# Three attention-and-MoE slots without weight conversions, and a reordered ending

## The chip, the cores and the metric

One core of one Trainium2 chip. The metric is the time of one execution in device microseconds (us); below is better. A core has TensorE (PE, matrix products; PEld its weight loads), VectorE (DVE), ScalarE (ACT), GpSimd (POOL) and SyncE (SP, which here issues every DMA). Each engine takes its instructions in the order in which the program issues them and waits for the others by semaphores.

## The reference

Sliding-window attention with a few global keys, and then two feed-forward layers over all 1,536 tokens (width 512, hidden width 2,048), all in float32:

```python
h = x @ w_in
g = np.maximum(h, 0.0) + alpha * np.minimum(h, 0.0)
x = (g @ w_out).astype(np.float32)          # first layer

h = x @ w_in                                # second layer
h2 = h * h
h3 = h2 * h
P = a[0] + a[1] * h + a[2] * h2 + a[3] * h3
Q = 1.0 + np.abs(b[0]) * np.abs(h) + np.abs(b[1]) * h2
g = P / (Q + 1e-06)
out = (g @ w_out).astype(np.float32)
```

## The kernel before

The two layers are cut into 96 **steps** (`plan_weights`, L221): a step is one layer, one group `g` of 512 tokens and one chunk of 128 hidden units. Steps 0 to 47 are the first layer, 48 to 95 the second. Precision comes from splitting every operand into a high and a low half and adding three products. A step has a **first product** (`first`, L731, matmuls of L738: 12 of 128x512 into one of banks 0 to 2), an elementwise part and a **second product** (`second`, L791, matmuls of L804: 12 into banks 4 to 7, which add up over a run of steps).

After the attention the steps go through **slots** (`plain_slot`, L866, slots 16 to 97). Slot s issues the first product of step s, the elementwise work of steps s-1 and s-2, and the second product of step s-2. In the second layer this is, for the step n: ACT L756, L757 and L761 read the bank (`rational_a`, `rational_u`); DVE L765 (`rational_b`); ACT L769 and L770 (`rational_c`); DVE L775 and L776 (`rational_p`); one slot later DVE L780, L781 and L782 (`rational_d`), ACT L785, which makes the high half `ghi` (`rational_h`), and POOL L789, which makes the low half `glo` (`rational_e`). The second product begins with `ghi` and takes `glo` in its last third.

Each slot has two **ticks** (`tick`, L284), numbered 2s and 2s+1: the first stands between L765 and L769, the second after the second product. The 20 ticks -20 to -1 run before slot 0. Ticks carry two sorts of side work:

- A **conversion** unpacks a chunk of weights that came in as 64-bit numbers. It is spread over four ticks: at tick t ACT scales it (L324), at t+1 DVE joins the bits (L313, L314, L315, and then the next load is issued on SP), at t+2 ACT makes the high half (L301), at t+3 DVE the low half (L304). `plan_weights` lists the ticks at which conversions begin; the last eight begin at 101, 106, ... 136 (L248), so 101 is the second tick of slot 50.
- The queue `later` holds the **low halves of the last sums** of a first-layer group that was computed in two runs of steps (those that end at steps 39 and 47): `drain` (L813) adds the bank to the saved part (DVE L829), ACT makes the high half (L837), and the low half (DVE L838, four of 128x512 per group) is queued. One is taken at every tick.

The ends of other runs (steps 55, 63, 79, 87, 95) copy or add banks 4 to 7 and store them: three drains at once, the fourth in the next slot.

The last step, 95, is done in halves of 256 tokens (`final_slot`, L899), since nothing is left to overlap it with; `drain` then adds the last bank in two halves (L825) and stores each with a DMA issued by SP (L826). The whole is in one arm of a run-time branch, so each engine ends its work with a branch (L92) and a closing sequence (L973).

Of the kernel before, what the change touches and what calls it, by code (L numbers as in the profile page):

```python
# [52 lines left out]
def flat(t):  # L53
    return t.rearrange("p c f -> p (c f)")


def words(t):
    return flat(t).bitcast(F32)


class Kernel:
# [35 lines left out]
    def arm(self, attention, sfx):  # L97
        tc = self.tc
        self.sfx = sfx
        self.slots = list(self.early)  # L100
        self.pipe, self.join, self.unspilled, self.later, self.splits = (deque() for _ in range(5))
        self.loads = self.started = self.used = 0
        moe = self.moe()
        with tc.tile_pool(name="spill_" + sfx, bufs=1, space=DRAM) as spill:
            self.spilled = [self.alloc_slot(spill, i, "d") for i in range(KEPT)]
            self.saved = {mg: spill.tile([P, NC, DM], F32, name=f"saved{mg[0]}{mg[1]}_{sfx}") for mg in SAVED}
            with tc.tile_pool(name="at_" + sfx, bufs=1) as pool:
                attention(pool, moe)
            with tc.tile_pool(name="late_" + sfx, bufs=1, reuse_waits="tile") as late:
                self.slots += [self.alloc_slot(late, i) for i in range(NEARLY, NF)]  # L110
                moe(None)
# [109 lines left out]
    def plan_weights(self):  # L221
        self.steps = [(0, 0, fc, fc % NEARLY) for fc in range(CH)]
        self.steps += [(0, 1, fc, fc % NEARLY) for fc in (*range(NEARLY, CH), *range(NEARLY))]
        self.steps += [(0, 2, fc, fc) for fc in range(NF)]
        self.steps += [(0, g, fc, fc) for g in (0, 1) for fc in range(CH, NF)]
        self.steps += [(1, g, j, j) for g in (2, 0) for j in range(CH)]
        self.steps += [(1, 1, j, j) for j in range(NF)]
        self.steps += [(1, g, j, j) for g in (2, 0) for j in range(CH, NF)]
        runs = [s[:2] for s in self.steps]
        self.begins = {n for n in range(len(runs)) if n == 0 or runs[n - 1] != runs[n]}  # L230
        self.ends = {n - 1 for n in self.begins if n} | {len(runs) - 1}
        self.saves = {n for n in self.ends if runs[n] in runs[n + 1 :]}
        self.adds = {n for n in self.ends - self.saves if runs[n] in SAVED}
        jobs = {}
        for fc in range(CH):
            jobs[2 * fc - 5 if fc > 2 else 2 * fc - 10] = 0, fc, "in", fc % NEARLY
            jobs[2 * fc - 2 if fc else -5] = 0, fc, "out", fc % NEARLY
        half, layer = NGR * CH, NGR * NF
        spare = [(fc, kind) for fc in range(CH, NF) for kind in ("in", "out")]
        for t, (fc, kind) in enumerate(spare):  # L240
            jobs[11 + 2 * t if fc < KEPT else 15 + 2 * t] = 0, fc, kind, None if fc < KEPT else fc
        todo = []
        for n, free in ((0, LATE), (CH, layer - CH)):
            for k in range(CH):
                for kind, lag in (("in", 0), ("out", 5)):
                    todo.append((n + k, 2 * (free + k) + lag, kind))
        times = [t for t in range(48, 96) if (t % 2 == 0 or t in (55, 71) or t > 82) and t not in (64, 66, 80, 82, 85, 88, 91, 94, 95)]
        times += range(101, 160, 5)  # L248
        for t in times:
            ready = [x for x in todo if x[1] <= t]  # L250
            if ready:
                j, _, kind = job = min(ready)
                todo.remove(job)
                jobs[t] = 1, j, kind, j
        assert not todo
        self.starts = set(jobs)
        self.plan = [jobs[t] for t in sorted(jobs)]
# [25 lines left out]

    def tick(self, on_act, start, spread=False):  # L284
        nc = self.nc
        if self.later:
            self.later.popleft()()
        while self.splits:
            self.splits.popleft()()
        self.join_step(5)  # L290
        if self.pipe and self.pipe[0][0] == "joined":
            _, n = self.pipe.popleft()
            m, fc, kind, slot = self.plan[n]
            self.spill()
            x = words(self.dx[n % 3])
            if slot is None:
                hi, lo = (t.bitcast(F32R) for t in self.part[1:3])
            else:
                hi, lo = (flat(self.slots[slot][kind, part]) for part in PARTS)
            if on_act:  # L300
                nc.scalar.copy(hi, x)  # L301
            else:
                nc.gpsimd.tensor_scalar(hi, x, 1.0, 1.0, ALU.mult, ALU.mult)
            self.splits.append(lambda: nc.vector.tensor_sub(lo, x, hi.bitcast(F32)))  # L304
            if m == 0 and fc < KEPT:
                for part, of in zip(PARTS, (hi, lo)):
                    self.unspilled.append((words(self.spilled[fc][kind, part]), of.bitcast(F32)))
        if self.pipe:
            _, n = self.pipe[0]
            self.pipe[0] = "joined", n  # L310
            low, e, y = self.staged(n)[:, :, :, 0], self.de[n % 2].bitcast(I32), self.dx[n % 3]
            self.join += [
                lambda: nc.vector.tensor_scalar(y, e, 3, None, ALU.logical_shift_left),  # L313
                lambda: nc.vector.scalar_tensor_tensor(y, e, -(2**31), y, ALU.bitwise_and, ALU.bitwise_or),  # L314
                lambda: nc.vector.scalar_tensor_tensor(y, low, 29, y, ALU.logical_shift_right, ALU.bitwise_or),  # L315
                self.load_more,
            ]
        if not spread:
            self.join_step(5)
        if start:  # L320
            n = self.started
            self.started += 1
            self.pipe.append(("scaled", n))
            nc.scalar.mul(self.de[n % 2], self.staged(n)[:, :, :, 1].bitcast(F32), 2.0**-112)  # L324
# [399 lines left out]
    def moe(self):  # L724
        nc, steps, banks = self.nc, self.steps, self.banks
        N = len(steps)
# [4 lines left out]
        def first(n):  # L731
            m, g, fc, slot = steps[n]
            w = self.slots[slot]
            bk = banks[3 if n < LATE else n % 3]
            seq = [(a, b, c) for a, b in (("hi", "hi"), ("lo", "hi"), ("hi", "lo")) for c in range(NC)]
            for e, (a, b, c) in enumerate(seq):
                x = (self.xhi if b == "hi" else self.xlo)[g]
                nc.tensor.matmul(bk, w["in", a][:, c, :], x[:, c, :], start=e == 0, stop=e == len(seq) - 1)  # L738
            hbank[n] = bk
# [73 lines left out]
        def drain(n, d):  # L813
            m, g = steps[n][:2]
            y, o, r0 = banks[4 + d], self.part[d], g * GT + d * P
            out = self.out[r0 : r0 + P, :]
            if n in self.saves:
                if n < LATE - 1:
                    o = self.first_saved[d]
                (nc.vector.tensor_copy if d == 3 and m else nc.scalar.copy)(o, y)  # L820
                nc.sync.dma_start(out=self.saved[m, g][:, d, :], in_=o)
                return
            if n == N - 1 and d == 3:
                for half in (slice(0, DM // 2), slice(DM // 2, DM)):
                    nc.vector.tensor_add(o[:, half], y[:, half], o[:, half])  # L825
                    nc.sync.dma_start(out=out[:, half], in_=o[:, half])  # L826
                return
            if n in self.adds:
                nc.vector.tensor_add(o, y, o)  # L829
            elif m:  # L830
                (nc.vector.tensor_copy if d == 3 else nc.scalar.copy)(o, y)
            if m:
                nc.sync.dma_start(out=out, in_=o)
                return
            xh, xl = self.xhi[g][:, d, :], self.xlo[g][:, d, :]
            if n in self.adds:
                nc.scalar.copy(xh, o)  # L837
                self.later.append(lambda: nc.vector.tensor_sub(xl, o, xh.bitcast(F32)))  # L838
            else:
                nc.scalar.copy(xh, y)  # L840
                nc.vector.tensor_sub(xl, y, xh.bitcast(F32))
# [24 lines left out]
        def plain_slot(s):  # L866
            early, late = s - 1, s - 2
            fetch(s + 1)
            if CH <= s - LATE + CH - 2 < KEPT:
                self.reload(s - LATE + CH - 2)  # L870
            if s < N:
                first(s)
            if s >= N:
                final_slot(s)
                return
# [102 lines left out]
```

## Time and profile before

| | |
|---|---|
| three runs shown | 676.52, 677.80 and 678.18 us, median 677.8 |
| the profiled execution's own time | 678.08 us |
| its span, first to last instruction | 676.2 us, so 1.9 us lie around it |
| mean granted TensorE clock | 0.98 |
| PE busy | 631.6 us, 93% of the span |
| DVE busy | 541.6 us, 80% |
| ACT busy | 374.7 us, 55% |
| POOL busy | 195.2 us, 29% |

Matmuls are pipelined: in an unbroken row they start 0.227 us apart, though a row of the profile gives each 0.39 us. So a slot of 24 matmuls takes 5.44 us, and idle time that the profile gives before a matmul is 0.16 us less than what is lost from start to start. In a timeline row a bracket tells how long the engine was idle before it and which instruction ended that.

### The profile page before, as it was taken

What the parts mean: (1) busy time and instruction counts of PE and PEld (TensorE: products, weight loads), DVE (VectorE), ACT (ScalarE), POOL (GpSimd) and SP (SyncE); (2) the same over time, 40 slices, a digit from 0 to 9 for tenths busy, and PEclk for the clock granted to TensorE, in tenths of its full rate; (3) what the DMA queues carried; (4) which work ended last, traced back from release to release, by engine and by line L of the source; (5) the groups of instructions that cost most, each with busy time, mean ns of one, the idle gap of its engine ahead of it and who ended that gap; (6) DMA issues with size and microseconds to landing.
All of it is one profiled execution on the core that took longest, in us unless ns stands there. A gap on an engine that the chain in (4) does not pass through costs nothing.

```text
span 676.2 us, 9567 instructions
## 1 busy us (share of the span) xinstructions
PE 631.6 (93%) x3250; PEld 510.2 (75%) x3250; DVE 541.6 (80%) x982; ACT 374.7 (55%) x782; POOL 195.2 (29%) x278
## 2 busy tenths in 40 slices
PE   7767998998988999999999998999999999999994
PEld 6656766776866888888888876888878888888782
DVE  3687789984654998876879999999999877786984
ACT  2775565665552432333324367777777766766662
POOL 4554334333232322222222212222222222222221
PEclk9897999998999999999999999999999999999997
DMA  8969488876667882331342231121110000300302
GB/s 164 198 165 271 136 249 251 258 221 222 186 225 235 291 317 89 99 121 31 126 155 63 70 117 31 32 95 39 55 62 1 1 1 1 124 1 0 126 0 69
DMA packets 84860, 82.83 MB, mean 123 GB/s; under 512 B 45312, under 2 KB 61952, under 8 KB 84800
## 3 DMA queue, kind: packets, MB, share of 16 engines
q1 hardware_dynamic: 84800, 82.11, 40.5%
q8 instruction: 28, 0.46, 0.3%
q14 instruction: 32, 0.26, 0.1%
HBM read 60.21 MB, written 19.92 MB: 119 GB/s over the span
## 4 chain that ended last, share of the span: by engine, by line
PE 59%; DVE 23%; ACT 6%; DMA 4%; issue 3%; POOL 3%; SPq 0%; DVEq 0%; ACTq 0%; POOLq 0%
PE bank L804 29%; PE bank L738 28%; DVE dx L314 3%; DVE dx L315 3%; DVE dx L313 3%; ACT prob L453 2%; DMA dwouthi_f<-part 2%; DVE prob L446 1%; DVE act L745 1%; DVE act L744 1%; DMA dwinhi_f<-part 1%; DVE xlo L527 1%; DVE klo L407 1%; DVE act L782 1%; POOL glo L747 1%
## 5 line engine op out<-in xcount | busy, mean ns | idle before, releaser
L747 POOL TENSOR_TENSOR glo<-act,ghi 128x512 fp32r<-128x512 f32 x48 | 65.6, 1367 | 225.6 <-ACT ghi L746 202.6
L789 POOL TENSOR_TENSOR glo<-act,ghi 128x512 fp32r<-128x512 f32 (+1 forms) x49 | 65.7, 1340 | 202.1 <-ACT ghi L785 187.2
L746 ACT CAST ghi<-act 128x512 fp32r<-128x512 f32 x48 | 29.8, 621 | 107.6 <-DVE act L745 99.7
L738 PE MATMUL bank<-xhi,winhi_f 128*128 128x512 f32 x256 | 68.4, 389 | 0.0
L738 PE MATMUL bank<-xhi,winlo_f 128*128 128x512 f32 x256 | 68.4, 389 | 0.0
L738 PE MATMUL bank<-xlo,winhi_f 128*128 128x512 f32 x256 | 68.4, 389 | 0.0
L453 ACT ACTIVATE prob<-prob,stat 128x232 f32<-128x232 f32 (+1 forms) x96 | 44.6, 466 | 38.8 <-DVE stat L446 38.7
L738 PEld LDWEIGHTS bank<-xhi,winhi_f 128*128 128x128 f32 x256 | 48.0, 188 | 10.0
L738 PEld LDWEIGHTS bank<-xlo,winhi_f 128*128 128x128 f32 x256 | 48.0, 188 | 10.0
L738 PEld LDWEIGHTS bank<-xhi,winlo_f 128*128 128x128 f32 x256 | 48.0, 188 | 10.0
L315 DVE SCALAR_TENSOR_TENSOR dx<-stage,dx 128x512 int32<-128x512 int32 x64 | 53.5, 836 | 2.2
L314 DVE SCALAR_TENSOR_TENSOR dx<-de,dx 128x512 int32<-128x512 int32 x64 | 51.8, 809 | 2.2
L756 ACT ACTIVATE stage<-bank 128x512 f32<-128x512 f32 (+1 forms) x49 | 28.8, 588 | 37.5 <-PE bank L738 37.4
L765 DVE SCALAR_TENSOR_TENSOR stage<-stage,abs_b 128x512 f32<-128x512 f32 (+1 forms) x49 | 36.2, 739 | 16.3 <-ACT stage L757 16.3
L470 POOL TENSOR_SCALAR prob<-prob,rec 128x232 f32<-128x232 f32 (+1 forms) x96 | 43.0, 464 | 21.7 <-DVE rec L465 14.3
L785 ACT CAST ghi<-act 128x512 fp32r<-128x512 f32 (+1 forms) x49 | 30.1, 614 | 26.5 <-DVE act L782 26.4
L324 ACT ACTIVATE de<-stage 128x512 f32<-128x512 f32 x64 | 42.4, 667 | 2.3 <-DMA stage<-in_moe_w_out_dram 2.3
L804 PE MATMUL bank<-wouthi_f,ghi 128*128 128x512 f32 x144 | 41.3, 392 | 0.6 <-ACT ghi L785 0.6
L744 DVE TENSOR_SCALAR act<-bank,al 128x512 f32<-128x512 f32 x48 | 35.8, 745 | 7.4 <-PE bank L738 7.2
L804 PE MATMUL bank<-wouthi_f,glo 128*128 128x512 f32 x144 | 41.2, 391 | 0.1
L804 PE MATMUL bank<-woutlo_f,ghi 128*128 128x512 f32 x144 | 41.0, 389 | 0.0
L313 DVE TENSOR_SCALAR dx<-de 128x512 int32<-128x512 int32 x64 | 38.0, 594 | 3.5 <-ACT de L324 3.5
(206 smaller groups left out, 1483.5 us busy)
## 6 DMA issues: line engine op xcount, KB each, us to landing
stage<-in_moe_w_in_dram SPq DMA_DIRECT2D x32, 512.0 KB, 4.1
stage<-in_moe_w_out_dram SPq DMA_DIRECT2D x32, 512.0 KB, 4.0
part<-saved_f SPq DMA_DIRECT2D x16, 256.0 KB, 4.3
va<-in_v_dram SPq DMA_DIRECT2D x13, 256.0 KB, 5.0
saved_f<-part SPq DMA_DIRECT2D x12, 256.0 KB, 3.7
out_dram<-part SPq DMA_DIRECT2D x11, 256.0 KB, 2.1
rawk<-in_k_dram SPq DMA_DIRECT2D x10, 256.0 KB, 4.7
rawq<-in_q_dram SPq DMA_DIRECT2D x10, 256.0 KB, 4.6
```

What stands on the lines that cost most here:

```text
L313: lambda: nc.vector.tensor_scalar(y, e, 3, None, ALU.logical_shift_left),
L314: lambda: nc.vector.scalar_tensor_tensor(y, e, -(2**31), y, ALU.bitwise_and, ALU.bitwise_or),
L315: lambda: nc.vector.scalar_tensor_tensor(y, low, 29, y, ALU.logical_shift_right, ALU.bitwise_or),
L324: nc.scalar.mul(self.de[n % 2], self.staged(n)[:, :, :, 1].bitcast(F32), 2.0**-112)
L453: nc.scalar.activation(p[:, j - e, :w], p[:, j - e, :w], AF.Exp, bias=st[:, j : j + 1], scale=-1.0, accum_out=st[:, 4 + j : 5 + j],)
L470: nc.gpsimd.tensor_scalar(p[:, j, :w], p[:, j, :w], r[:, e + j : e + j + 1], 1.0, ALU.mult, ALU.mult)
L738: nc.tensor.matmul(bk, w["in", a][:, c, :], x[:, c, :], start=e == 0, stop=e == len(seq) - 1)
L744: nc.vector.tensor_scalar(t, h, 0.0, self.al[:, fc : fc + 1], ALU.min, ALU.mult)
L747: nc.gpsimd.tensor_tensor(lo, t, hi.bitcast(F32), ALU.subtract)
L765: nc.vector.scalar_tensor_tensor(w, w, self.ab[:, 0:1], ab, ALU.add, ALU.mult)
L789: nc.gpsimd.tensor_tensor(lo, u, hi.bitcast(F32), ALU.subtract)
L804: nc.tensor.matmul(y[d], lhs, rhs, start=begin and e == 0, stop=last and e == 2)
```

## The change

Four edits. A counter of ticks is kept, and `later` is served only when it is odd. The last eight conversions begin at ticks 107, 112, ... 142. Of the two half stores of the last drain, ACT issues the second. In slot 94 the first products of steps 94 and 95 are issued one after the other, and slot 95 issues none.

```diff
-        self.loads = self.started = self.used = 0
+        self.loads = self.started = self.used = self.ticks = 0
...
-        times += range(101, 160, 5)
+        times += range(107, 160, 5)
...
-        if self.later:
+        self.ticks += 1
+        if self.later and self.ticks % 2:
             self.later.popleft()()
...
-                    nc.sync.dma_start(out=out[:, half], in_=o[:, half])
+                    (nc.scalar if half.start else nc.sync).dma_start(out=out[:, half], in_=o[:, half])
...
-            if s < N:
+            if s < N - 1:
                 first(s)
+            if s == N - 2:
+                first(s + 1)
```

## Rows read from the trace of the kernel before

**Rows 1.** Spans and clock of the core.
```profile
core 0: 676.2 us, clock 0.980
```

**Rows 2.** Windows: stretch, its length, busy us (count) of PE, PEld, DVE, ACT, POOL, clock, DMA.
```profile
410.00:420.00 10.00, 8.15 (x36) 6.40 (x35) 9.79 (x15) 5.54 (x9) 2.21 (x2) 1.00 0.18 52
...
420.00:424.00 4.00, 4.00 (x12) 3.12 (x11) 3.89 (x6) 2.88 (x6) 1.04 (x1) 0.57 0.00 0
...
560.00:570.00 10.00, 10.00 (x46) 8.29 (x45) 8.01 (x12) 6.34 (x11) 2.59 (x2) 1.00 0.00 0
```

**Rows 3.** Timeline of PE in slots 50 to 53: start, us, instruction, times, [idle before].
```profile
406.23 1.19 PE L804 MATMUL bank<-wouthi__113,ghi 128*128 128x512 f32 x4 [1.50 <-ACT ghi L785]
...
416.42 1.07 PE L738 MATMUL bank<-xlo,winhi_f 128*128 128x512 f32 x4
419.34 1.47 PE L804 MATMUL bank<-wouthi__121,ghi 128*128 128x512 f32 x4 [1.85 <-ACT ghi L785]
...
423.78 1.09 PE L738 MATMUL bank<-xhi,winhi_f 128*128 128x512 f32 x4
```

**Rows 4.** Chain that ended last, 400 to 430 us: start, us, what.
```profile
402.76 0.60 DVE xlo L838
...
411.60 0.60 DVE xlo L838
412.20 1.45 DVE dx L313
...
413.67 0.70 DVE dx L314
...
414.40 0.69 DVE dx L315
```

**Rows 5.** Timeline of ACT in slot 50.
```profile
404.38 0.78 ACT L761 ACTIVATE act<-bank,na 128x512 f32<-128x512 f32 x1
405.56 0.62 ACT L785 CAST ghi<-act 128x512 fp32r<-128x512 f32 x1 [0.40 <-DVE act L782]
```

**Rows 6.** Timelines of DVE and POOL, side work beside and apart from POOL's subtraction.
```profile
411.72 1.63 POOL L789 TENSOR_TENSOR glo<-act,ghi 128x512 fp32r<-128x512 f32 x1 [3.77 <-ACT ghi L785]
...
440.09 1.70 POOL L789 TENSOR_TENSOR glo<-act,ghi 128x512 fp32r<-128x512 f32 x1 [3.48 <-issue]
...
440.67 1.67 DVE L315 SCALAR_TENSOR_TENSOR dx<-stage,dx 128x512 int32<-128x512 int32 x1
...
482.74 0.69 DVE L315 SCALAR_TENSOR_TENSOR dx<-stage,dx 128x512 int32<-128x512 int32 x1
```

**Rows 7.** Timeline of PE, slots 59 and 67.
```profile
458.26 1.07 PE L738 MATMUL bank<-xlo,winhi__123 128*128 128x512 f32 x4
459.41 1.20 PE L804 MATMUL bank<-wouthi__117,ghi 128*128 128x512 f32 x4
...
504.49 1.21 PE L804 MATMUL bank<-wouthi__117,ghi 128*128 128x512 f32 x4 [0.80 <-ACT ghi L785]
```

**Rows 8.** Timeline of all engines in the last two slots.
```profile
657.35 0.75 DVE L782 SCALAR_TENSOR_TENSOR act<-act,na,stage 128x512 f32<-128x512 f32 x1
...
657.70 0.38 ACT L756 ACTIVATE stage<-bank 128x256 f32<-128x256 f32 x1 [1.88 <-PE bank L738]
...
659.57 0.48 DVE L765 SCALAR_TENSOR_TENSOR stage<-stage,abs_b 128x256 f32<-128x256 f32 x1 [0.61 <-ACT stage L757]
...
660.56 1.20 PE L804 MATMUL bank<-wouthi_f,ghi 128*128 128x512 f32 x4 [0.18 <-ACT ghi L785]
```

**Rows 9.** SP at the end, by line: duration ns min/median/max, first and last start.
```profile
L826 SPq DMA_DIRECT2D out_dram<-part x2: 883/1030/1177, 667.9 to 669.2; - x2
...
L833 SPq DMA_DIRECT2D out_dram<-part x11: 332/337/338, 582.3 to 667.5; - x11
...
L92 SPq COMPARE_BRANCH  x2: 46/48/49, 6.9 to 670.1; - x2
...
L973 SPq EVENT_SEMAPHORE  x10: 17/28/28, 673.0 to 676.1; - x10
```

## The prediction

> **What bounds the kernel now.** I read the spans first [rows 1]: one core, clock 0.98, so there is almost no lost clock to win back except where the windows show it. Then the windows: PE works without a break around 560 us, where DVE is busy 8.0 of 10 us, but it has gaps between 400 and 424 us, where DVE is busy 9.8 of 10, and the granted clock falls to a mean of 0.57 between 420 and 424 [rows 2]. The reader should see two regimes: PE sets the pace where DVE has room, DVE where it has side work. A slot's matmuls take 5.44 us; DVE's own work is 0.801 x 5.44 = 4.4 us a slot, so 1.1 us is all the room for side work.
>
> The timeline of PE shows where DVE wins: the second products of slots 50 and 52 wait for the high half `ghi` [rows 3]. From start to start the first wait loses 1.50 + 0.16 = 1.66 us, and the second 419.34 - (416.42 + 4 x 0.227) = 2.01 us. After the second, the 12 matmuls take 423.78 - 419.34 = 4.44 us instead of 2.72, so 1.72 us goes to TensorE running at 1.2 instead of 2.4 GHz, right behind that idle stretch. After the shorter wait of slot 50 no fall is seen. The chain of waits runs through DVE the whole time between the two [rows 4]: four low halves L838 of 0.60 us, and the joins L313 to L315 of the conversion begun at tick 101, 1.45 + 0.70 + 0.69 = 2.84 us. Those are what the change moves.
>
> **Part 1: ticks.** Two ticks a slot and 20 before slot 0 make the counter odd at the first tick of a slot. So the low half that was taken at 402.76 us, between the sums and L780 of step 48, moves behind that work. The chain loses 0.60 us there, but ACT's L761 runs to 405.16 us ahead of `ghi`, which started at 405.56 [rows 5], and in the closest rows the next ACT instruction starts at about the end of the one before. I take 0.5 us (ends 0.4 and 0.6). Slot 50 still waits about 1.15 us.
>
> By 418 us two of the four low halves are gone from the chain (1.2 us) and all three joins (2.84 us): DVE delivers step 50 about 4.0 us earlier, while PE asks 0.5 us earlier. The 2.01 us wait disappears with 1.5 us in reserve. The clock fell only behind that wait, so its 1.72 us goes too; a wait shorter than the 1.66 us that brought no fall stays in slot 50. **Slots 50 to 52: 0.5 + 2.0 + 1.7 = 4.2 us gained.** From below: if the clock falls anyhow, 2.5.
>
> The low halves of the other group, which ends at step 39, also spread, over slots 42 to 45. I cost this at nothing: DVE does no more up to any tick than before, and PE's second products hide it. If that cover were gone it would be 0.6 us once. The load for step 47 overwrites the same tiles; it is issued on SP in slot 46, a slot after the last low half, and is needed in slot 49, three slots or 16 us later.
>
> **Part 2: the conversions come three slots later.** Nothing is saved: eight conversions of five DVE and two ACT instructions each, with their loads behind L315 on SP, still have to run, now up to slot 72. Their inputs are staged long before, and the weights are not needed before step 76. Joins fall by turns into a first tick, beside POOL's subtraction, where one of them takes 1.67 us, or into a second tick, where it takes 0.69 [rows 6]; the split is four and four before and after. What differs is how they meet the extra copies at the ends of steps 55 and 63. Before, step 55 met a conversion begun at the first tick of slot 58, and PE waited 0.24 us in slot 59, with some 0.14 lost in the start behind it (1.20 against 1.07); step 63 met one begun at the second tick of slot 65, and slot 67 waited 0.80 + 0.16 = 0.96, again with 0.14 [rows 7]. Together 1.48. After, step 63 meets one begun at the first tick of slot 66, which is the old position of step 55: 0.38 us. Step 55 meets one begun at the second tick of slot 58, joined in 59, a slot after the copy. No row shows that position; it lies between 0 and twice the worst seen, 2.2, and I take 0.5, nearer to the cases in which copy and join fall into different slots. **Gain 1.48 - 0.88 = 0.6 us** (ends -1.1 and 1.1).
>
> A rule bears on this. In slot 51 L838 starts at 411.60, just before POOL's subtraction at 411.72, which takes 1.63 us; in slot 56 POOL starts at 440.09, DVE's join at 440.67, and it is the join that takes 1.67 instead of 0.69 [rows 4, 6]. The Trainium skill (SBUF — State Buffer, "Who interferes with whom") says that a DVE instruction with two SBUF inputs and a GpSimd instruction that reads SBUF exclude each other for the whole instruction, and that whichever issues first makes the other wait. The trace agrees. By that rule the new places of all four low halves, at first ticks, are the bad ones; by the rows DVE comes first there and POOL alone is held, which has until the last third of the second product. So the sum has no term for it, and the other order is a rival.
>
> **Part 3: the ending.** Step 95's first product goes ahead of the second product of step 92; PE's total and the place of second product 93 are the same. Its bank was last read in slot 93. ACT now stands idle 1.88 us for that product, and DVE, free from L782 at 658.10, gets its second L765 only at 659.57 [rows 8]. With the product 2.72 us earlier, ACT does this work behind step 94's, and DVE runs both halves of L765 from 658.1: the second starts at 658.5 to 658.6. All DVE work behind it follows without a gap to the last sum, so the last sum comes 1.0 to 1.1 us earlier; the small wait of the second product of step 94 (0.18 + 0.16) goes with it. I take 1.1.
>
> The two half stores occupy SP for 1.18 and 0.88 us, one after the other, against 0.34 for a full one; SP's branch follows at 670.1 and its closing waits start at 673.0 [rows 9]. With the second store on ACT, which has nothing left to do, SP's branch comes one issue earlier: 0.9 to 1.2 us, and I take 1.0. ACT pays 0.34 to 1.18 us for it, behind which only its own branch and closing stand. From below nothing is gained, when the landings set the end. **Ending: 2.1 us.**
>
> **Sum.** 4.2 + 0.6 + 2.1 = 6.9 us of the profiled execution's 678.08 (span 676.2 and 1.9 around it), which stands 0.3 above the median of 677.8: 671.2 there, 670.9 as a median.
>
> **The rivals.** (a) *The second queue brings nothing* because the last transfer sets the end. For it: the long issues look held back by what is already under way [rows 9]. Against: SP's closing waits begin 2.9 us after its branch, which leaves that long for landings. 670.9 + 1.0 = 671.9 us. The Trainium skill (DMA: Bandwidth & Descriptors, "Issuing engines are not separate DMA queues") says the same DMA engines serve all issuers, so only the sequencer's issue time is saved; no row here shows two issuers.
>
> (b) *The low halves lose to POOL.* If POOL starts first, each L838 takes 1.0 us more (1.67 - 0.69). The two ahead of step 50 then cost 2.0 against 1.5 in reserve, the two in slots 52 and 53 make DVE's slot 4.4 + 0.6 + 1.0 = 6.0 us against 5.44, and the conversions start with less reserve, some 0.3 more: 0.5 + 2 x 0.55 + 0.3 = 1.9, so 672.8 us.
>
> (c) *Paid later.* DVE is full to 520 us; what slots 50 to 52 gain comes back as waits when the conversions run to slot 72, and only the ending stays: 677.8 - 2.1 = 675.7 us. Against it: three free slots give DVE room first, and 560 to 570 us shows 2 us of room per 10 [rows 2].
>
> (d) *Slower.* The three later conversions that are joined beside POOL (slots 59, 64, 69) each leave DVE over 2 us late one slot on, as in slot 52, with the fall of the clock: 3 x (2.01 + 1.72) = 11.2 us lost. With 4.2 and 2.1 gained and the old 1.48 gone: 677.8 - 7.8 + 11.2 = 681.2 us. It decides at 2 us; the old joins of that kind after slot 53 left waits up to 0.96.
>
> **How the numbers follow.** Forecast 0.66, (a) 0.13, (b) 0.12, (c) 0.06, (d) 0.03. The range: 0.9 of remaining later waits, 0.8 at the end (a full store's 0.34 instead of a half's 1.18) and 0.2 of slot 50's wait could go, 669.0; upward it takes in (a), and (b) with 0.8 of the unknown position, 673.6. It leaves out (c), (d) and little else. A measurement tells some 0.3%, 2.0 us, from no change. Forecast, (a), (b) and half of (c) are faster by more: 0.94; half of (c) is within, 0.03; (d) 0.03.
>
> **What would show it.** Right: PE waits some 1.2 us in slot 50, not at all in 52; the clock is 1.00 from 400 to 440 us; no L313 between 400 and 422 us; PE waits in all under 1.2 us from slot 53 to 73; ACT's L756 of step 95 follows its L770 without idle time; SP's branch comes 2 us earlier against its last matmul's old place. Wrong: a wait over 1.7 us or a clock below 1.00 between 400 and 540 us; L838 of 1.6 us; a closing whose waits begin where they did relative to the last sum.

## The result and the profile after

The median is 671.08 us (670.93 to 671.30) against 677.75 before, a ratio of 0.9905 with a 95% interval of 0.9888 to 0.9922. The forecast was 670.9 us in a range of 669.0 to 673.6.

The profiled execution took 671.30 us. The head of the changed kernel's page and its part 1 (busy us, share, instructions):

```profile
span 669.4 us, 9568 instructions
...
PE 630.1 (94%) x3250; PEld 511.4 (76%) x3250; DVE 540.6 (81%) x982; ACT 375.3 (56%) x782; POOL 195.4 (29%) x278
```

The span is 6.8 us shorter than that of [rows 1], with DVE's work the same to 1 us: 541.6 before, 540.6 now. Nothing was removed; work was moved. Three stretches of the changed kernel, the ones of [rows 2] (columns as there):

```profile
410.00:420.00 10.00, 10.00 (x46) 8.29 (x45) 9.79 (x16) 7.61 (x13) 3.26 (x2) 1.00 0.00 0
420.00:424.00 4.00, 4.00 (x20) 3.30 (x19) 3.89 (x7) 3.50 (x7) 1.63 (x1) 1.00 0.02 4
...
560.00:570.00 10.00, 10.00 (x45) 8.27 (x45) 7.76 (x11) 7.06 (x12) 2.59 (x2) 1.00 0.01 2
```

DVE is as full as before between 410 and 424 us, but what fills it is now the elementwise work that PE waits for: PE has 46 and 20 matmuls there instead of 36 and 12, and the clock stays at 1.00. The timeline of PE shows the two second products that answer to [rows 3]:

```profile
406.09 1.20 PE L805 MATMUL bank<-wouthi__113,ghi 128*128 128x512 f32 x4 [1.12 <-ACT ghi L786]
...
417.12 1.07 PE L805 MATMUL bank<-wouthi__121,ghi 128*128 128x512 f32 x4
```

Slot 50 waits 1.12 + 0.16 = 1.28 us instead of 1.66, slot 52 not at all (no bracket).

To tell where time goes in all runs, I use the start of four first products in the timeline of PE, of the steps 49, 53, 74 and 94, and the end of the span. Without any wait a slot takes 5.44 us, so the second column would be 21.76, the third 114.24 and their sum 136.00. What lies ahead of step 49 took 395.6 to 398.9 us in these executions, in no order that follows the edits, so spans are compared by these stretches and not as wholes.

| kernel | 49 to 53 | 53 to 74 | sum | 74 to 94 | 94 to end |
|---|---|---|---|---|---|
| before | 27.38 | 116.26 | 143.64 | 109.30 | 26.85 |
| changed | 23.19 | 115.72 | 138.91 | 109.32 | 24.53 |
| changed again | 23.15 | 115.67 | 138.82 | 109.36 | 24.54 |
| shift only | 23.62 | 115.71 | 139.33 | 109.33 | 26.73 |
| spread only | 24.73 | 119.75 | 144.48 | 109.31 | 26.63 |
| first product early | 27.27 | 116.33 | 143.60 | 109.38 | 25.52 |
| ACT store | 25.80 | 117.39 | 143.19 | 109.37 | 25.93 |
| one conversion a tick earlier | 23.17 | 114.93 | 138.10 | 109.35 | 24.48 |
| all at first ticks | 23.17 | 114.24 | 137.41 | 109.35 | 24.45 |
| sums later | 22.59 | 116.22 | 138.81 | 109.33 | 24.49 |
| both stores on ACT | 23.17 | 115.72 | 138.89 | 109.33 | 23.28 |
| whole store | 23.16 | 115.68 | 138.84 | 109.36 | 23.74 |
| combined | 22.55 | 114.24 | 136.79 | 109.33 | 23.15 |
| combined, whole store | 22.54 | 114.24 | 136.78 | 109.36 | 23.34 |

So the change gained 4.19 us in slots 49 to 52 (from the first product of 49 to that of 53), 0.54 up to step 74, nothing from there to step 94, and 2.32 at the end. The two executions of the changed kernel differ by at most 0.09 us in a stretch. The ending is less sure: one and the same ending took 26.85 us in the kernel before, 26.73 with the shift only and 26.63 with the spread only.

A wait of the changed kernel that was not forecast stands in slot 65. Its timeline:

```profile
485.23 1.07 PE L739 MATMUL bank<-xhi,winhi__115 128*128 128x512 f32 x4
...
487.35 0.68 DVE L305 TENSOR_TENSOR winlo_f<-dx,winhi_f 128x512 fp32r<-128x512 f32 x1
...
487.56 1.62 POOL L790 TENSOR_TENSOR glo<-act,ghi 128x512 fp32r<-128x512 f32 x1 [5.62 <-ACT ghi L786]
...
488.18 0.39 PE L805 MATMUL bank<-woutlo_f,ghi 128*128 128x512 f32 x1
...
489.23 0.50 PE L805 MATMUL bank<-wouthi_f,glo 128*128 128x512 f32 x1 [0.67 <-POOL glo L790]
```

Step 63 ends a run, so its second product finishes one bank after the other and takes `glo` at its third matmul, not in its last third. PE waits 0.67 us inside the product, and the 12 matmuls take 0.98 us more than 2.49 from first to last start. Two things make `glo` late. POOL, which usually takes 1.3 us, takes 1.62 beside the conversion's low half L305; and it starts late, 2.33 us behind the slot's first matmul, because `ghi` comes late. The first alone makes no wait. At the end of step 55, in slot 57, the profiled kernel before has the same meeting and no wait (timelines of PE and POOL):

```profile
445.56 1.07 PE L738 MATMUL bank<-xhi,winhi__115 128*128 128x512 f32 x4
...
446.66 1.63 POOL L789 TENSOR_TENSOR glo<-act,ghi 128x512 fp32r<-128x512 f32 x1 [4.88 <-ACT ghi L785]
...
448.74 0.39 PE L804 MATMUL bank<-wouthi_f,glo 128*128 128x512 f32 x1
```

POOL takes 1.63 us there too, but starts 1.10 us behind the slot's first matmul. In the changed kernel, slot 67 loses another 0.39 us: the product starts there at 500.03 us, and 0.22 of that is a wait.

### The profile page after: what moved, and what is told of

Read it like the earlier page. It is cut to its first block, busy times and chain, and to the rows that moved or that the text cites. A ratio compares the mean times of both kernels' runs of the same rounds, so it can differ in the third digit from the quotient of the medians.

```text
span 669.4 us, 9568 instructions
## 1 busy us (share of the span) xinstructions
PE 630.1 (94%) x3250; PEld 511.4 (76%) x3250; DVE 540.6 (81%) x982; ACT 375.3 (56%) x782; POOL 195.4 (29%) x278
## 5 line engine op out<-in xcount | busy, mean ns | idle before, releaser
L315 DVE SCALAR_TENSOR_TENSOR dx<-de,dx 128x512 int32<-128x512 int32 x64 | 53.7, 839 | 2.2
L316 DVE SCALAR_TENSOR_TENSOR dx<-stage,dx 128x512 int32<-128x512 int32 x64 | 51.6, 806 | 2.2
L766 DVE SCALAR_TENSOR_TENSOR stage<-stage,abs_b 128x512 f32<-128x512 f32 (+1 forms) x49 | 36.1, 738 | 12.4 <-ACT stage L758 12.4
L786 ACT CAST ghi<-act 128x512 fp32r<-128x512 f32 (+1 forms) x49 | 30.2, 616 | 28.2 <-DVE act L783 28.1
```

Source lines behind the costliest of these rows:

```text
L766: nc.vector.scalar_tensor_tensor(w, w, self.ab[:, 0:1], ab, ALU.add, ALU.mult)
```

## The experiments

### The four parts alone

*Shift only* (the conversions begin at 107, nothing else changes):

```diff
-        times += range(101, 160, 5)
+        times += range(107, 160, 5)
```

> The conversions alone begin at tick 107; low halves, first products and stores as before. Theory (DVE's chain between 402 and 419 us sets the waits of slots 50 and 52): slot 50 still waits 1.66 us, since nothing ahead of it changes; the joins' 2.84 us leave the chain ahead of step 50, more than the 2.01 us wait, so slot 52 waits not at all and the clock stays at 1.00 there (1.72 us); with about 0.5 at the later ends of runs as in the changed kernel, 4.2 us faster than before, 673.5 us. Rival (the low halves are what holds slot 52): a wait of 1 us or more stays there, and with it half-clock time: 1 to 2.5 us faster.

Measured: 674.08 us against 678.38 for the kernel before beside it, 0.9936 (0.9922 to 0.9950). From the timeline of PE:

```profile
405.42 1.21 PE L804 MATMUL bank<-wouthi__113,ghi 128*128 128x512 f32 x4 [1.48 <-ACT ghi L785]
...
416.51 1.07 PE L804 MATMUL bank<-wouthi__121,ghi 128*128 128x512 f32 x4
...
488.62 0.50 PE L804 MATMUL bank<-wouthi_f,glo 128*128 128x512 f32 x1 [0.67 <-POOL glo L789]
```

Slot 50 waits 1.48 + 0.16 = 1.64 us as before, slot 52 not at all, and the new wait of slot 65 is there too: it belongs to the shift. The theory held, the rival fell. The shift alone takes 4.31 us out of the sum of both stretches (143.64 to 139.33).

*Spread only* (low halves at first ticks, conversions as before):

```diff
+        self.ticks += 1
-        if self.later:
+        if self.later and self.ticks % 2:
```

> The low halves alone are taken at first ticks only; conversions at 101, 106, ... as before. Theory: slot 50 waits about 0.4 to 0.5 us less; two low halves (1.2 us) leave the chain ahead of step 50, so slot 52 waits about 2.01 + 0.5 - 1.2 = 1.3 us. If the fall of the clock hangs on the length of that wait, it does not come behind 1.3 us (slot 50's 1.66 us brought none), and the gain is 0.5 + 0.7 + 1.7 = 2.9 us, 674.8 us. Rival (any second wait after slot 50's brings the fall): 1.2 us faster, 676.5 us.

Measured: 679.30 us against 678.38, 1.0008 (0.9996 to 1.0019): no gain, and neither forecast was right. The clock did not fall in the profiled execution, and the second products that wait, by the timeline of PE, are these:

```profile
406.49 1.20 PE L805 MATMUL bank<-wouthi__113,ghi 128*128 128x512 f32 x4 [1.11 <-ACT ghi L786]
...
418.92 1.20 PE L805 MATMUL bank<-wouthi__121,ghi 128*128 128x512 f32 x4 [1.24 <-ACT ghi L786]
425.44 1.20 PE L805 MATMUL bank<-wouthi__125,ghi 128*128 128x512 f32 x4 [0.76 <-ACT ghi L786]
432.04 1.20 PE L805 MATMUL bank<-wouthi_f,ghi 128*128 128x512 f32 x4 [0.81 <-ACT ghi L786]
...
450.13 0.50 PE L805 MATMUL bank<-wouthi_f,glo 128*128 128x512 f32 x1 [1.01 <-POOL glo L790]
```

Slots 50 and 52 wait less, as forecast, and slots 53, 54 and 57 wait in their place. A low half that is put off by a slot is still DVE's work in a stretch where DVE has none to spare: it is paid later, to the full (sum 144.48 against 143.64). What was rival (c) for the whole change is true of this part alone.

*First product early* (the order in slot 94) and *ACT store* (the second half store):

```diff
-            if s < N:
+            if s < N - 1:
                 first(s)
+            if s == N - 2:
+                first(s + 1)
```

> The order of the last two first products alone. Theory: DVE's second half of L765 and all behind it come 1.1 us earlier, and the last sum, SP's branch and the end with it: 1.1 to 1.3 us faster, 676.5 us. Rival (the end is set by landings or by code that is loaded behind the branch, whenever the sums come): under 0.3 us.

Measured: 676.64 us, 0.9977 (0.9967 to 0.9986); the last stretch is 25.52 us instead of 26.85, 1.33 less (1.1 to 1.3 less than the three executions with the ending of before). The theory held.

```diff
-                    nc.sync.dma_start(out=out[:, half], in_=o[:, half])
+                    (nc.scalar if half.start else nc.sync).dma_start(out=out[:, half], in_=o[:, half])
```

> The second half store alone is issued by ACT. Theory: SP's branch comes one issue (0.9 us) earlier and the end follows: 0.9 us faster, 676.8 us; ACT's issue takes 0.4 us as in the changed kernel. Rival (landings set the end): the closing's last wait stays where it was and nothing is gained.

Measured: 677.23 us, 0.9984 (0.9972 to 0.9997); the last stretch is 0.92 us shorter (0.7 to 0.9 against the same three). This too held. The run tells something else as well, because its middle is that of the kernel before. Timeline of PE:

```profile
408.73 1.21 PE L804 MATMUL bank<-wouthi__113,ghi 128*128 128x512 f32 x4 [1.48 <-ACT ghi L785]
...
421.84 1.21 PE L804 MATMUL bank<-wouthi__121,ghi 128*128 128x512 f32 x4 [1.87 <-ACT ghi L785]
...
450.76 0.50 PE L804 MATMUL bank<-wouthi_f,glo 128*128 128x512 f32 x1 [0.93 <-POOL glo L789]
```

and the windows of the same execution (columns as in [rows 2]):

```profile
420.00:424.00 4.00, 2.16 (x9) 1.79 (x10) 3.93 (x7) 2.75 (x5) 1.63 (x1) 1.00 0.21 73
424.00:428.00 4.00, 4.00 (x19) 3.30 (x19) 3.90 (x7) 2.88 (x6) 1.26 (x1) 1.00 0.00 0
```

The same two waits, 1.64 and 2.03 us, and this time the clock stays at 1.00 behind them: the first stretch takes 25.80 us instead of 27.38. But slot 57 now waits 0.93 us that it did not wait before, since POOL starts there 2.61 us behind the slot's first matmul (449.10 against 446.49 us) instead of 1.10, and the sum of both stretches is 143.19 against 143.64. *First product early*, which has the same middle too, had the fall (a clock of 0.57 from 420 to 424 us), no wait in slot 57, and a sum of 143.60. What fits all three: while PE runs at half clock, DVE, which is full, catches up; without that it is late later on. So the fall of the clock, 1.72 us by itself, costs some 0.4 us net, and it came in two of the three profiled executions with this middle. Against the one without it the shift still gains 143.19 - 139.33 = 3.86 us, so the fall is not what the shift lives on.

### The new wait, and the places of the conversions

*One conversion a tick earlier*, on top of the change:

```diff
+        times[times.index(127)] = 126
```

> The changed kernel, with the conversion of tick 127 begun at 126, so that its low half L305 falls into the second tick of slot 64 instead of the first of slot 65, and its joins into a second tick. Theory (the new wait of 0.98 us inside the second product of slot 65 comes from POOL's subtraction, held by L305, while a run's last step takes glo at its third matmul): that wait shrinks to under 0.5 us, POOL's subtraction there takes 1.3 instead of 1.62 us, and slot 67 loses no more than its 0.4: 0.5 to 1.0 us faster than the changed kernel, 670.3 us. Rival (glo is late there because ghi is late, whatever DVE does beside it): unchanged, 671.1 us.

Measured: 670.58 us against 678.03, 0.9884 (0.9868 to 0.9901). That interval overlaps the changed kernel's, so the profile has to decide: the product of slot 65 loses 0.19 instead of 0.98 us, and the stretch 53 to 74 falls by 0.79 us. Timelines of PE and POOL:

```profile
486.00 1.07 PE L740 MATMUL bank<-xhi,winhi__115 128*128 128x512 f32 x4
...
487.84 1.30 POOL L791 TENSOR_TENSOR glo<-act,ghi 128x512 fp32r<-128x512 f32 x1 [3.52 <-ACT ghi L787]
```

The numbers are those of the theory, but its cause is only part of it, because the edit moves the joins too: one of them took 1.67 us in slot 64 of the changed kernel (480.83 us) and takes 0.69 here. POOL's subtraction is 0.32 us shorter, and it starts 0.49 us earlier behind the slot's first matmul (1.84 instead of 2.33). So the rival, a late `ghi`, was right for the larger part.

*All at first ticks*, on top of the change: each conversion then joins its bits and makes its low half in second ticks, away from POOL.

```diff
-        times += range(107, 160, 5)
+        times += (108, 112, 118, 122, 126, 134, 138, 142, 146, 150)
```

> The changed kernel, with all eight conversions begun at first ticks (108, 112, 118, 122, 126, 134, 138, 142), so that all joins and low halves of weights fall into second ticks, away from POOL. Theory: no join takes 1.67 us any more (four times 1.0 us of DVE saved), and no second product between slots 53 and 73 waits: the 1.48 us that the changed kernel still loses there (0.1 in slot 60, 0.98 in 65, 0.4 in 67) goes: 669.7 us. Rival (the copies at the ends of runs make the waits, not the joins' places): 0.4 in slot 67 and most of slot 65's wait stay, 670.8 us.

Measured: 669.89 us against 678.03, 0.9878 (0.9862 to 0.9895). The joins L315 and L316 between 420 and 540 us, first of the changed kernel, by line (duration ns min/median/max):

```profile
L315 DVE SCALAR_TENSOR_TENSOR dx<-de,dx x8: 691/693/1670, 425.6 to 522.6; 128x512 int32<-128x512 int32 x8
...
L316 DVE SCALAR_TENSOR_TENSOR dx<-stage,dx x8: 691/692/1664, 426.3 to 523.4; 128x512 int32<-128x512 int32 x8
```

and then of this one:

```profile
L315 DVE SCALAR_TENSOR_TENSOR dx<-de,dx x8: 692/693/693, 427.2 to 520.4; 128x512 int32<-128x512 int32 x8
...
L316 DVE SCALAR_TENSOR_TENSOR dx<-stage,dx x8: 691/692/694, 428.0 to 521.2; 128x512 int32<-128x512 int32 x8
```

No join takes 1.67 us any more, and the stretch 53 to 74 takes 114.24 us, 21 slots of 5.44: every wait in it is gone, by the places of the conversions alone. The copies at the ends of runs, the rival, cost nothing once DVE has this room.

*Sums later*, on top of the change: the last sums of step 47 wait in the queue of drains, which is served behind L781 to L783 of step 48.

```diff
-                if m == 0 or n == N - 1 or d < 3:
+                if (m == 0 and n != LATE * 3 - 1) or n == N - 1 or (m and d < 3):
```

> The changed kernel, with the four last sums of step 47 (L830) and their high halves issued behind L781 to L783 of step 48 instead of ahead of them. Theory: ghi of step 48 no longer stands behind four sums (2.4 us) and four high halves, slot 50 waits not at all (1.28 us less), and DVE, which has the same work, gives some of it back as a wait of up to 0.4 us in slot 51: 0.9 to 1.3 us faster than the changed kernel, 670.0 us. Rival (the second product of slot 50 then waits for the banks that the sums must free): no gain or a loss of 0.5 us.

Measured: 670.76 us, 0.9898 (0.9881 to 0.9914), not told apart from the changed kernel. Timeline of PE:

```profile
404.27 1.11 PE L805 MATMUL bank<-wouthi__113,ghi 128*128 128x512 f32 x4
...
410.34 1.19 PE L805 MATMUL bank<-wouthi__117,ghi 128*128 128x512 f32 x4 [0.40 <-ACT ghi L786]
...
444.01 0.50 PE L805 MATMUL bank<-wouthi_f,glo 128*128 128x512 f32 x1 [0.21 <-POOL glo L790]
```

Slot 50 no longer waits, as the theory said, but slot 51 waits 0.56 us and slot 57 loses 0.54: 22.59 us in the first stretch (0.60 less) and 116.22 in the second (0.50 more). The forecast of 0.9 to 1.3 us was a miss, for the reason seen in the spread: the gain is paid later while DVE is full.

### The ending

*Both stores on ACT*, on top of the change:

```diff
-                    (nc.scalar if half.start else nc.sync).dma_start(out=out[:, half], in_=o[:, half])
+                    nc.scalar.dma_start(out=out[:, half], in_=o[:, half])
```

> The changed kernel, with both half stores issued by ACT. Theory (SP's issue of a half takes 1.2 us because SP's queue still holds the stores ahead of it, ACT's 0.4): both issues take about 0.4 us on ACT, SP's branch comes 1.4 us earlier, and ACT's, at about 663.0, becomes the last: up to 0.6 us faster than the changed kernel, 670.5 us. Rival (a half store costs 1.2 us wherever a second one is under way, or the landings set the end now): ACT's second issue takes about 1.2 us or the closing's last wait stays, and nothing is gained.

Measured: 669.55 us against 678.03, 0.9876 (0.9859 to 0.9892); the last stretch takes 23.28 us, 1.25 less than the changed kernel's. Issues and branches by line (duration ns, first and last start), first of the changed kernel:

```profile
L827 SPq DMA_DIRECT2D out_dram<-part x1: 1278/1278/1278, 662.2 to 662.2; - x1
...
L827 ACTq DMA_DIRECT2D out_dram<-part x1: 374/374/374, 662.5 to 662.5; - x1
...
L92 SPq COMPARE_BRANCH  x2: 41/45/49, 7.0 to 663.6; - x2
```

and of this one:

```profile
L827 ACTq DMA_DIRECT2D out_dram<-part x2: 379/728/1077, 661.7 to 662.2; - x2
...
L92 ACTq COMPARE_BRANCH  x2: 38/42/45, 6.8 to 663.3; - x2
L92 SPq COMPARE_BRANCH  x2: 41/45/49, 7.1 to 661.7; - x2
```

Half of the theory and half of the rival: a half store takes 0.38 us as ACT's first and 1.08 as its second, and ACT branches at 663.3. Yet the gain is twice the 0.6 us that was forecast, because ACT's branch does not set the end. SP's does: from its branch to the end of the span pass 6.0 us before (670.1 to 676.2), 5.9 in the changed kernel (663.55 to 669.41), and 6.0 here (661.7 to 667.7). A landing does not set the end either: the last store landed 4.0 us ahead of it in the changed kernel and 2.5 us ahead of it here.

*Whole store*, on top of the change: the last bank is added at once and stored by one full-width DMA of SP.

```diff
-                for half in (slice(0, DM // 2), slice(DM // 2, DM)):
+                for half in (slice(0, DM),):
...
-                    (nc.scalar if half.start else nc.sync).dma_start(out=out[:, half], in_=o[:, half])
+                    nc.sync.dma_start(out=out[:, half], in_=o[:, half])
```

> The changed kernel, with the last bank added at once and stored by one full-width DMA of SP. Theory A (SP's fourth store is held back by the three ahead of it): its issue takes about 1.2 us, as the half's did, SP's branch comes 0.2 to 0.3 us later than in the changed kernel because the add ends later, and the time is 0 to 0.4 us longer. Theory B (the narrow pieces of a half store are what costs): it takes 0.34 us like the other full ones, SP's branch comes 0.6 us earlier, and the time is 0.6 us shorter than that of the changed kernel.

By line, this kernel's last issue and SP's branch (its span is 670.4 us):

```profile
L827 SPq DMA_DIRECT2D out_dram<-part x1: 332/332/332, 664.2 to 664.2; - x1
...
L92 SPq COMPARE_BRANCH  x2: 41/45/49, 7.1 to 664.6; - x2
```

The whole store's issue takes 0.33 us behind three others, where the half store took 1.28: theory B, it is not the stores ahead alone that hold it. The last stretch is 0.79 us shorter, and SP's branch lies 5.8 us ahead of the end. In the runs (671.01 us, 0.9894, 0.9875 to 0.9912) this cannot be told from the changed kernel beside it, *changed again*:

> The changed kernel again, beside the three above on one chip, so that they can be compared with it: a ratio to the kernel before of 0.9905, within its interval of 0.9888 to 0.9922.

Measured: 671.47 us against 678.31, 0.9907 (0.9890 to 0.9924), as expected.

### Together

*Combined* is the change with the conversions at first ticks, the later sums and both stores on ACT; *combined, whole store* has one full-width store on ACT in place of the two halves.

> The changed kernel with three edits of the earlier runs together: conversions begun at first ticks, the sums of step 47 behind L781 to L783 of step 48, both half stores on ACT. Theory (DVE has room from slot 53 on once no join meets POOL, so what slot 50 saves is not paid back): the waits of slots 53 to 73 stay gone (114.2 us from the first product of step 53 to that of step 74), slots 50 to 52 lose 0.9 instead of 1.4, the ending is that of both stores on ACT, 23.3 us from the first product of step 94: 3.2 us faster than the changed kernel, 667.9 us where the changed kernel has 671.1. Rival (DVE is still the bound there, so the savings don't add up): 2 us or less.

> As the combined kernel, with the last bank added at once and stored by one full-width DMA of ACT. If a second store in a row costs 1.1 us on whatever queue, one issue of 0.4 us replaces 0.4 and 1.1: ACT's branch 0.7 to 0.9 us earlier and the time 0.3 to 0.9 us shorter than the combined kernel's. If the last landing or SP's closing sets the end instead, the same time or, by the later start of the store, 0.3 us longer.

Measured, beside *changed again*: 668.25 us, 0.9857 (0.9835 to 0.9879), and 667.57 us, 0.9838 (0.9818 to 0.9859), against 671.47. The combined kernel is 3.2 us faster than the change by the medians, as forecast: the first stretch keeps the 0.6 us of the later sums and the second stays at 114.24 us, so with room on DVE the saving is no longer paid back. The two combined kernels cannot be told apart. In the profiles the last stretch with the whole store is 0.2 us longer, and SP's branch stands 5.9 and 6.1 us ahead of the end; that ACT has one issue fewer brought nothing, as one would expect when SP's branch sets the end. Both beat the kernel before and the changed one.

## Why the prediction was right, point by point

**The time and its sum.** 6.9 us were forecast and 6.7 measured by the medians. Of the terms, slots 50 to 52 were put at 4.2 us and gave 4.19 (49 to 53), the later slots at 0.6 and gave 0.54, the ending at 2.1 and gave 2.32. The first two matches are closer than the reasons for them, and in part luck, as the next points show.

**Slot 50**, 0.5 us: it gained 1.66 - 1.28 = 0.38, a little under the lower end of 0.4. ACT set it, as argued: L762 starts at 404.76 us and L786 at 405.42, right behind it. By itself this part gained nothing; on top of the shift it takes 0.42 us out of both stretches (139.33 to 138.91).

**Slot 52**, 2.0 + 1.7 us: the wait went and 1.53 us of reserve is what the trace shows against 1.5 forecast (`ghi` of step 50 ends at 415.59, the product starts at 417.12). But the reason given for the clock was wrong in one step: "The clock fell only behind that wait, so its 1.72 us goes too". With the same wait the ACT-store run had no fall, and paid 1.13 of the 1.58 us in later waits. Measured against that run, the first stretch gains 2.61 us and the second 1.67: the split of the forecast holds only because the profiled execution had the fall, and the sum, 4.28 instead of 4.73, moves less. Where DVE is the bound, time that PE loses there is not added to the total, and a wait that ends is paid later. That the sum still came out is owed to the room: the conversions end three slots later, where DVE has 1.1 us to spare in each slot, so by estimate 3 x 1.1 = 3.3 us of DVE's work leave the full stretch. The shift alone measured 4.3 us, the spread alone -0.8. The statement that held is the first one, that DVE sets the pace there; the change works by stretching that regime, not by clearing two waits.

**The later slots**, 1.48 to 0.88 us: that the gain came out at 0.54 for 0.6 is luck, since both sides were read too low by about the same. The kernel before lost 116.26 - 114.24 = 2.02 us there, not 1.48: slot 66 lost another 0.40, in no term, because its product starts 0.23 us late and slowly. Timeline of PE:

```profile
496.78 1.07 PE L738 MATMUL bank<-xlo,winhi__119 128*128 128x512 f32 x4
497.92 1.19 PE L804 MATMUL bank<-wouthi__113,ghi 128*128 128x512 f32 x4
```

And the changed kernel lost 1.48 us, not 0.88. Step 63's meeting, for which a row of before stood, was put at 0.38 us and measured 0.39 (slot 67). Step 55's, for which none stood, was put at 0.5 and cost 0.1 (slot 60). The 0.98 us of slot 65 were in no term. The step that failed is "by the rows DVE comes first there and POOL alone is held, which has until the last third of the second product". It is true of the four low halves, beside which POOL's subtractions took 1.56 to 1.64 us and no product waited for them. It is not true of a step that ends a run when DVE is late as well, since that product asks for `glo` at its third matmul. The rows of before did not show that wait: their execution had the fall of the clock, and the ACT-store run, without it, waits 0.93 us in the same position. The Trainium skill (SBUF — State Buffer, "Who interferes with whom") names the exclusion of DVE and POOL; the traces agree with it, 1.62 us on POOL beside L305 against 1.30 apart from it. What neither told is who waits for POOL.

**The ending**, 1.1 + 1.0 us: alone the two parts gave 1.33 and 0.92 us. L766's two halves follow L783 at once, and the last second product starts without a wait. The timeline of all engines in the changed kernel, for [rows 8]:

```profile
651.27 0.38 ACT L757 ACTIVATE stage<-bank 128x256 f32<-128x256 f32 x1
...
653.57 0.88 DVE L766 SCALAR_TENSOR_TENSOR stage<-stage,abs_b 128x256 f32<-128x256 f32 x2
...
655.76 1.07 PE L805 MATMUL bank<-wouthi_f,ghi 128*128 128x512 f32 x4
...
658.48 0.39 PE L805 MATMUL bank<-wouthi_f,ghi 128*128 128x512 f32 x1
```

**The rivals.** (a) The landings do not set the end: it follows SP's branch by 5.8 to 6.1 us in all fourteen profiled executions, and the last landing by 2.5 to 4.2 us. (b) did not happen: L839 takes 0.69 us at each new place. (c) is true of the spread alone and not of the shift. (d) stayed far away: the largest loss of a slot after slot 53 is 0.98 us, and the clock stayed at 1.00 from 209 us on until the last sums were done.

## What to carry to other kernels

Where one engine is full over a stretch, a wait that another engine loses to it is no sum that can be taken out: count the full engine's work in the whole stretch, and look for edits that carry work out of it to where there is room; moving work inside it only moves the wait. Look at which side work shares a time with POOL, at what makes POOL's input late, and at which product asks for POOL's result first: putting eight conversions at other ticks removed every wait of 21 slots. At the end, ask which engine's closing comes last, and give that engine the least to issue.

## What was not expected of the hardware

- The end of the span stands 5.8 to 6.1 us behind SP's branch in all fourteen profiled executions, whatever ACT still had to issue, while the last store landed 2.5 to 4.2 us ahead of the end. Between SP's branch and its first closing wait pass 2.5 to 3.5 us (663.6 to 666.2 us in the changed kernel, 660.5 to 664.0 in the last of the combined ones). The Trainium skill (Runtime: NRT & Kernel Launch, "Instruction fetch mechanics") says that a taken branch breaks the sequential loading of code. The pause fits that, but no run tells this cause apart from others: with the whole store and in both combined kernels the first closing wait stands only 0.1 to 0.2 us behind the landing of the last store.
- A half-width store took its issuer 0.37 to 0.38 us as the first on ACT's queue, 0.7 to 1.1 us as the second there, and 0.8 to 1.3 us on SP behind other stores. A full-width one took 0.33 to 0.58 us, behind others on SP or alone on ACT.
- With the same idle stretch of 2.0 us ahead of it, the clock fell in the kernel before and in the run with the first product early, and stayed at 1.00 in the ACT-store run.
